# A scale vector loaded as rows, two small jobs moved to ScalarE, and other fill counts in an attention and MLP kernel

## The chip, the cores and the metric

The kernel runs on one core of a Trainium2 chip (trn2). The metric is the device time of one execution in microseconds (us), lower is better. Before the change it took 330.53 us (median of three runs, 330.24 to 331.06). A difference counts as faster or slower from 2% on, which is 6.6 us here.

## The reference

Nyström attention with 32 landmarks over (8 batches, 8 heads, 576 positions, 64), then one MLP block with a layer norm. The landmarks are means over 18 neighbours; the inverse of the 32x32 matrix comes from six iterations.

```python
A  = sm(q, k_lm);  Bm = sm(q_lm, k_lm);  C = sm(q_lm, k)     # sm: scaled softmax
Z  = Bm.T / (norm1(Bm) * norminf(Bm) + 1e-06)
for _ in range(6):
    Z = 2 * Z - Z @ Bm @ Z
x  = heads_side_by_side(A @ Z @ C @ v)                       # (8, 576, 512)
xn = (x - mean) / sqrt(var + 1e-06) * g_ln                   # g_ln: 512 numbers
return x + relu(xn @ w_ch1) @ w_ch2                          # 512 -> 2048 -> 512
```

## The kernel before

One program does both. TensorE (PE in the profile) has the most work. Attention runs in "sets" of batches; between two of its steps, `fill(n)` puts n pieces of the MLP's product stream into PE's order, so that PE has work while the other engines finish a step. At the very start there is no MLP work yet, and `warm(...)` issues products of zeros instead. The MLP works on groups of four blocks of 128 rows: `psh` is the first product of a block group, `pso` the second. `pscv` is C @ v, `psb` the scores of the landmarks, with which a set's iterations begin, and `psy` the last product of attention; `pszc` is the last product of the iterations, `zcbd` what VectorE makes of it as the input of `psy`; `st` and `ebd` are VectorE's tiles between the iterations' products, and `xblk` is a block of attention's result. `xn` is the normalised input, and `xnT` its turned copy, made by PE for the first groups and by a transposing DMA later.

The scale vector g is folded into W1. It is needed with one number for each partition, and it is loaded that way, as a 128x4 tile in pieces of 4 bytes, in the queue of SyncE (SP) behind the loads of q, k and v for the first batch:

```python
load_qk(0)
load_v(0)
g_sb = wpool.tile([P, KCH], FP32, name="g_sb")
keep(nc.sync.dma_start(out=g_sb[:], in_=moe_g_ln.rearrange("(c p) -> p c", p=P)))
...
def cast_v(b):                                   # GpSimd, both halves
    natv_of[b] = natv = natv_buf[b % NV]
    for u in range(U):
        pool.tensor_copy(out=natv[:, 2 * u:2 * u + 2, :, 0:D], in_=raw[b]["v", u][:])
...
def scale_w1(i, by=(0, 1, 2, 3)):                # W1 * g: a quarter on VectorE, the rest on GpSimd
    for c in by:
        o, i_ = w1_16[:, c, ts(i, W1N)], w1_stg[i, c // 2][:, ts(c % 2, W1N)]
        if c == 0:
            dve.tensor_scalar(out=o, in0=i_, scalar1=g_sb[:, c:c + 1], scalar2=None, op0=ALU.mult)
        else:
            pool.tensor_scalar(out=o, in0=i_, scalar1=g_sb[:, c:c + 1], scalar2=0.0,
                               op0=ALU.mult, op1=ALU.add)
```

The turned copies, the stores of the results and the later loads share one queue, SyncE's, which issues one after another:

```python
def center(j):                                   # GpSimd makes xn of block j, then it is turned
    ...
    pool.tensor_scalar(out=xn_of[j][:], in0=x_blk[j][:], scalar1=1.0, scalar2=negm, ...)
    turn_by_dma(j)

def turn_by_dma(j):
    ...
    keep(nc.sync.dma_start(out=xnTs[g][:, :, ts(u, P)], in_=xn_of.pop(j)[:], transpose=True))
    turned[g].append(j)

def store(j, ot, cols=ds(0, DM), queues=(nc.sync, nc.sync)):
    for i in range(2):
        ...                                      # two half-stores of block j
```

The first unit and the fill counts (cut):

```python
for it in range(6):                              # the six iterations of the first batch
    run(a0)                                      # one step of attention
    warm(1, 512)                                 # a product of zeros
    if it == 5:
        scale_w1(0, (0,))                        # VectorE scales the first part of W1
...
counts = [[8, 13, 9] + 6 * [7] + [5] + 3 * [6] + 2 * [9],                       # set 2
          [10, 10, 9, 9, 9, 9] + [9, 9, 8, 8, 8, 8] + [8] + [8, 8, 6, 5] + 6 * [9],   # set 3+4
          ...]
```

The softmax here doesn't subtract the row's maximum and nothing guards it: scores larger than these inputs give would overflow.

Of the kernel before, what the change touches and what calls it, by code (L numbers as in the profile page):

```python
# [10 lines left out]
FP32 = mybir.dt.float32  # L11
UINT32 = mybir.dt.uint32
AF = mybir.ActivationFunctionType
# [3 lines left out]
P = 128  # L17
# [3 lines left out]
def kernel(  # L21
# [10 lines left out]
    nc = tc.nc  # L32

    B, H, S, D = q.shape
    DM = H * D
# [5 lines left out]
    KCH = DM // P  # L41
# [10 lines left out]
        name=nc.get_next_instruction_name(), act_func_set_id=6, ins=[], outs=[]))  # L52

    const = ctx.enter_context(tc.tile_pool(name="const", bufs=1))
    wpool = ctx.enter_context(tc.tile_pool(name="wpool", bufs=1))
    stage = ctx.enter_context(tc.tile_pool(name="stage", bufs=6))
    nat = ctx.enter_context(tc.tile_pool(name="nat", bufs=8))


    keep = tc.keep_in_program_order  # L60
# [8 lines left out]
    dve, pool, scalar = Ordered(nc.vector), Ordered(nc.gpsimd), Ordered(nc.scalar)  # L69
    act = scalar.activation  # L70

    def MM(o, l, r, rb=0, cb=0, start=True, stop=True, skip=False):
        keep(nc.tensor.matmul(o, l, r, start=start, stop=stop, tile_position=(rb, cb),  # L73
                              skip_group_check=(skip or cb != 0)))

    def TR(o, i_, idn):
        keep(nc.tensor.matmul(o, i_, idn, is_transpose=True, tile_position=(0, 0)))
# [9 lines left out]
    raw = {0: {}, 1: {}}  # L87
# [26 lines left out]
    def cast_v(b):  # L114
# [4 lines that stand above are left out]
    nat_tiles, natv_of = {}, {}  # L119
# [1 line left out]
    load_qk(0)  # L121
    load_v(0)
    g_sb = wpool.tile([P, KCH], FP32, name="g_sb")
    keep(nc.sync.dma_start(out=g_sb[:], in_=moe_g_ln.rearrange("(c p) -> p c", p=P)))

    zeros = const.tile([P, 128], FP16, name="zeros")
    nc.vector.memset(zeros[:], 0.0)

    ident16 = const.tile([P, P], FP16, name="ident16")
    make_identity(nc, ident16)  # L130


    pm16 = const.tile([P, 64], FP16, name="pm16")
# [38 lines left out]
    natv_buf = []  # L172
# [7 lines left out]
        zcbd_buf.append(t)  # L180


    cast_v(0)
    bones = const.tile([P, 4, 32], FP16, name="bones")
    for u in range(U):
        for nm in ("q", "k"):
# [13 lines left out]
    w1_16 = wpool.tile([P, KCH, HID], FP16, name="w1_16")  # L200
    w2_16 = wpool.tile([P, MCH, DM], FP16, name="w2_16")
    w1_src = moe_w_ch1.rearrange("(c p) f -> p c f", p=P)
    xpool = ctx.enter_context(tc.tile_pool(name="xpool", bufs=16))

    W1N = 256
    w1_stg = {}
# [11 lines left out]
    def scale_w1(i, by=(0, 1, 2, 3)):  # L218
        for c in by:
            o, i_ = w1_16[:, c, ts(i, W1N)], w1_stg[i, c // 2][:, ts(c % 2, W1N)]  # L220
            if c == 0:
                dve.tensor_scalar(out=o, in0=i_, scalar1=g_sb[:, c:c + 1],
                                  scalar2=None, op0=ALU.mult)
            else:
                pool.tensor_scalar(out=o, in0=i_, scalar1=g_sb[:, c:c + 1],
                                   scalar2=0.0, op0=ALU.mult, op1=ALU.add)
# [37 lines left out]
    psM = ctx.enter_context(tc.tile_pool(name="psM", bufs=3, space=bass.MemoryType.PSUM))  # L264


    def warm(n, cols):
        idle = psM.tile([P, 512], FP32, name="idle", tag="pm")
        for _ in range(n):
            MM(idle[:, 0:cols], zeros[:], zeros[:, None, :].broadcast_to([P, cols // P, P]))  # L270
# [596 lines left out]
    def mlp():  # L867
        for g in range(NGRP):
            mlp_at[0] = g
            hT = mhT.tile([P, MCH, 512], FP16, name="hT", tag="hT")  # L870
            if g == 0:
                for u in (0, 2):
                    if u == 0:
                        for i in range(2):
                            transpose_block(0, i)
                            yield True
                    for m0 in range(0, MCH, 2):
                        if u == 0 and m0 in (6, 10):
                            transpose_block(0, 2 if m0 == 6 else 3)
                            yield True  # L880
                        if u == 0 and m0 < MCH - 6:
                            scale_w1(m0 // 2 + 3)
                        psh = psM.tile([P, 2, 256], FP32, name="psh", tag="pm")
                        for m in range(2):
                            for c in range(KCH):
                                MM(psh[:, m, :], w1_16[:, c, ts(m0 + m, P)],
                                   xnTs[0][:, c, ds(P * u, 256)],
                                   start=(c == 0), stop=(c == KCH - 1), skip=True)
                                if c == 1 or (c == 3 and m == 0):
                                    yield True  # L890
                        act(hT[:, m0:m0 + 2, ds(P * u, 256)], psh[:], AF.Relu)
                        yield True
# [52 lines left out]
    def run(*who):  # L945
        for a in who:
            next(a)
# [5 lines left out]
    run(a0)  # L953
    warm(1, 512)
    run(a0)
    warm(1, 512)
    run(a0)
    warm(2, 512)
    for it in range(6):
        run(a0)  # L960
        warm(1, 512)
        if it == 5:
            scale_w1(0, (0,))
    run(a0)
# [3 lines left out]
    run(a1)  # L968
    warm(1, 512)
    scale_w1(0, (1, 2, 3))  # L970
    fill(1)
    warm(2, 512)
# [57 lines left out]
    for _ in range(2):  # L1030
# [1 line left out]


    counts = [[8, 13, 9] + 6 * [7] + [5] + 3 * [6] + 2 * [9],
              [10, 10, 9, 9, 9, 9] + [9, 9, 8, 8, 8, 8] + [8] + [8, 8, 6, 5] + 6 * [9],
              [12, 12, 15, 15, 15, 13] + 6 * [11] + [10] + 10 * [8],
              [14, 21, 21] + 6 * [10] + [10] + 5 * [9]]
    for c, after, count in zip(sets, sets[1:] + [None], counts):
# [46 lines left out]
```

## Time and profile before

| | before |
|---|---|
| median, three runs | 330.53 us |
| profiled execution, span | 328.4 us |
| PE busy | 314.6 us of the span |
| first `psy` (first product with attention's result) | 22.10 us |
| GpSimd's last `xn` of group 3 ends | 137.03 us |
| its turned copy is issued / PE's `psh` of group 3 starts | 139.19 / 142.17 us |
| last VectorE step starts | 324.44 us |

In a timeline of SyncE's queue the columns are start, length of the issue, queue, line, operation, out<-in, how many.

```profile
136.57 1.21 SPq L861 DMA_TRANSPOSE xnT<-xn  x1
137.87 1.23 SPq L820 DMA_DIRECT2D out_dram<-ot  x2
139.19 1.26 SPq L861 DMA_TRANSPOSE xnT<-xn  x1
```

GpSimd had finished xn of block 15 at 137.03. The queue was issuing the copy of block 14 then, and after it two half-stores, and only at 139.19 the copy of block 15: 2.16 us after its input was ready.

### The profile page before, as it was taken

How to read it: one execution, taken by the hardware profiler on the slowest of the kernel's cores; microseconds unless marked ns; L12 is line 12 of the kernel's file. 1: busy time of each engine (PE TensorE's matmuls, PEld its weight loads, DVE VectorE, ACT ScalarE, POOL GpSimd, SP SyncE). 2: the span in 40 equal slices, each digit the busy share in tenths (PEclk: the TensorE clock that was granted, in tenths of full speed). 3: DMA queues.
4: the chain of work that ended last, by engine and by line, in shares of the span. 5: the costliest groups of instructions: out<-in, count | busy, mean ns of one | idle time of the engine just before them, and what ended most of it. 6: DMA issues, size and time to landing. Idle time of an engine off the chain costs nothing.

```text
span 328.4 us, 8241 instructions
## 1 busy us (share of the span) xinstructions
PE 314.6 (96%) x3408; PEld 163.0 (50%) x3408; DVE 176.7 (54%) x396; ACT 150.9 (46%) x304; POOL 154.6 (47%) x240
## 2 busy tenths in 40 slices
PE   8879899999999999989999999999999999999995
PEld 8537764454445544434545445454444444444443
DVE  2658869879966588864228568822557120010012
ACT  2426762739961561867304664364046107305600
POOL 3489889999999999989900025200014000000000
PEclk9999999999999999999999999999999999999999
DMA  7999999998598683698022203230242125032023
GB/s 276 350 361 360 383 401 291 317 359 250 212 209 226 186 225 109 163 278 128 4 66 59 43 16 80 66 66 2 64 103 27 32 64 98 0 72 60 0 49 79
DMA packets 36917, 50.34 MB, mean 153 GB/s; under 512 B 18320, under 2 KB 22672, under 8 KB 36880
## 3 DMA queue, kind: packets, MB, share of 16 engines
q1 hardware_dynamic: 36720, 49.69, 53.1%
q8 instruction: 26, 0.43, 0.6%
q10 hardware_dynamic: 160, 0.13, 0.2%
q14 instruction: 11, 0.09, 0.1%
HBM read 36.70 MB, written 9.44 MB: 141 GB/s over the span
## 4 chain that ended last, share of the span: by engine, by line
PE 58%; POOL 17%; DVE 6%; DMA 4%; issue 3%; ACT 2%; SPq 0%; POOLq 0%
PE psh L73 27%; PE pso L73 25%; POOL asum L67 9%; POOL nat L67 4%; POOL natv L67 2%; DMA out_dram<-ot 2%; POOL xn L67 2%; PE psy L73 1%; ACT xn L67 1%; DMA stg<-in_v_dram 1%; PE pscv L73 1%; DVE xT L67 1%; DVE ebd L67 1%; POOL s L67 1%; DMA xnT<-xn 1%
## 5 line engine op out<-in xcount | busy, mean ns | idle before, releaser
L73 PE MATMUL psh<-xnT,w 128*128 128x512 f16 (+1 forms) x640 | 134.2, 358 | 1.0 <-DMA xnT<-xn 1.0
L73 PE MATMUL pso<-w,hT 128*128 128x512 f16 (+1 forms) x592 | 133.0, 374 | 0.0
L67 ACT ACTIVATE hT<-psh 128x512 f16<-128x512 f32 x144 | 84.7, 597 | 94.8 <-PE psh L73 94.6
L73 PEld LDWEIGHTS <-w 128*128 128x128 f16 x640 | 59.4, 98 | 56.0 <-issue 3.0
L73 PEld LDWEIGHTS <-hT 128*128 128x128 f16 x592 | 56.0, 98 | 57.8 <-issue 0.9
L67 DVE SCALAR_TENSOR_TENSOR ot<-pso,rstd,xblk 128x512 f32<-128x512 f32 (+1 forms) x37 | 27.1, 732 | 79.0 <-PE pso L73 78.9
L67 POOL CAST nat<-stg 128x1152 f16<-128x1152 f32 x28 | 32.9, 1185 | 3.8 <-DMA stg<-in_k_dram 1.2
L67 POOL TENSOR_TENSOR asum<-asum 128x256 f32<-128x256 f32 (+2 forms) x54 | 28.3, 523 | 4.2
L67 DVE TENSOR_TENSOR xblk<-psy,rcpd 128x512 f32<-128x512 f32 (+1 forms) x40 | 27.6, 691 | 1.7
L67 POOL TENSOR_TENSOR asum<-nat 128x576 f32<-128x576 f16 x18 | 24.9, 1381 | 1.5
L67 DVE SCALAR_TENSOR_TENSOR st<-st,psn 128x192 f16<-128x192 f16 (+3 forms) x36 | 14.2, 395 | 19.1 <-PE psn L73 19.1
L67 POOL TENSOR_SCALAR xn<-xblk,mvg 128x512 f16<-128x512 f32 x14 | 9.6, 695 | 30.3 <-ACT junk L67 30.3
L67 POOL CAST natv<-stg 128x1152 f16<-128x1152 f32 x16 | 18.1, 1150 | 9.6 <-DMA stg<-in_v_dram 9.6
L67 POOL TENSOR_SCALAR negm<-mvg 128x1 f32<-128x1 f32 x14 | 2.7, 191 | 41.7 <-DVE mvg L67 40.2
L67 DVE TENSOR_TENSOR ebd<-st,mask 128x256 f16<-128x256 f16 (+1 forms) x30 | 21.4, 715 | 1.0
L67 DVE STREAM_TRANSPOSE xT<-nat 128x576 uint32<-128x576 uint32 x24 | 18.2, 760 | 0.8 <-POOL nat L67 0.8
L73 PE MATMUL psy<-zcbd,ea 128*128 128x260 f16 (+1 forms) x80 | 15.9, 276 | 1.3 <-DVE zcbd L67 1.1
L67 ACT ACTIVATE ea<-psea 128x576 f16<-128x576 f32 x12 | 7.2, 648 | 17.8 <-PE psea L73 17.8
L73 PE MATMUL idle<-zeros 128*128 128x128 f16 (+2 forms) x82 | 14.0, 325 | 1.1 <-DVE eps_ln L167 1.1
L73 PEld LDWEIGHTS <-ea 128*128 128x128 f16 (+1 forms) x80 | 7.3, 100 | 11.9 <-issue 4.2
L67 DVE RECIPROCAL rcpd<-psy 128x8 f32<-128x8 f32 (+1 forms) x40 | 7.8, 195 | 9.9 <-PE psy L73 9.6
L67 ACT ACTIVATE junk<-xblk 128x512 f16<-128x512 f32 x14 | 8.8, 625 | 9.3 <-DVE xblk L67 9.1
(109 smaller groups left out, 265.5 us busy)
## 6 DMA issues: line engine op xcount, KB each, us to landing
stg<-in_q_dram SPq DMA_DIRECT2D x16, 576.0 KB, 6.2
stg<-in_k_dram SPq DMA_DIRECT2D x16, 576.0 KB, 6.0
out_dram<-ot SPq DMA_DIRECT2D x70, 128.0 KB, 2.4
stg<-in_v_dram SPq DMA_DIRECT2D x10, 576.0 KB, 8.2
w1stg<-in_moe_w_ch_dram SPq DMA_DIRECT2D x16, 256.0 KB, 6.0
w2stg<-in_moe_w_ch_dram SPq DMA_DIRECT2D x16, 256.0 KB, 5.4
stg<-in_v_dram SPq DMA_DIRECT2D x12, 288.0 KB, 5.7
xnT<-xn SPq DMA_TRANSPOSE x28, 3.2
```

The lines of the kernel that those rows point to most:

```text
L67: return lambda *args, **kw: keep(getattr(self.engine, op)(*args, **kw))
L73: keep(nc.tensor.matmul(o, l, r, start=start, stop=stop, tile_position=(rb, cb), skip_group_check=(skip or cb != 0)))
```

## The change

The intent: free the DMA engines of a load in 512 small pieces, take two short jobs off GpSimd's and VectorE's order in the opening, and shift MLP products in the set of batches 3 and 4. The tile `g_rows` borrows a buffer of a pool that had to move to an earlier place for it.

```diff
-    keep(nc.sync.dma_start(out=g_sb[:], in_=moe_g_ln.rearrange("(c p) -> p c", p=P)))
+    g_rows = xpool.tile([P, DM], FP32, name="g_rows", tag="xblk")[0:KCH, 0:P]
+    keep(nc.sync.dma_start(out=g_rows, in_=moe_g_ln.rearrange("(c p) -> c p", p=P)))
...
+    ident4 = const.tile([KCH, KCH], FP32, name="ident4")
+    nc.gpsimd.tensor_copy(out=ident4[:], in_=ident16[0:KCH, 0:KCH])
...
-    cast_v(0)
+    natv_of[0] = natv_buf[0]
+    pool.tensor_copy(out=natv_buf[0][:, 0:2, :, 0:D], in_=raw[0]["v", 0][:])
+    pool.tensor_copy(out=natv_buf[0][:, 2, :, 0:D], in_=raw[0]["v", 1][:, 0])
...
-            if c == 0:
+            if c == 0 and i == 0:
+                act(o, i_, AF.Copy, scale=g_sb[:, c:c + 1])
+            elif c == 0:
...
     warm(1, 512)
     run(a0)
+    scalar.copy(natv_buf[0][:, 3, :, 0:D], raw[0]["v", 1][:, 1])
...
     for it in range(6):
         run(a0)
         warm(1, 512)
+        if it == 2:
+            psg = psM.tile([P, KCH], FP32, name="psg", tag="pm")
+            TR(psg[:], g_rows, ident4[:])
+            scalar.copy(g_sb[:], psg[:])
...
-              [10, 10, 9, 9, 9, 9] + [9, 9, 8, 8, 8, 8] + [8] + [8, 8, 6, 5] + 6 * [9],
+              [10, 9, 9, 9, 9, 8] + [8, 9, 9, 8, 8, 8] + [8] + [8, 7, 5, 4] + 6 * [9],
```

## The prediction

> **What bounds the kernel now.** I read the page first, then the busy time by stretch, the timeline of the first 30 us, and the chain of waits. The page says TensorE (PE) is the bound:
>
> ```profile
> span 328.4 us, 8241 instructions
> PE 314.6 (96%) x3408; PEld 163.0 (50%) x3408; DVE 176.7 (54%) x396; ACT 150.9 (46%) x304; POOL 154.6 (47%) x240
> ```
>
> PE is idle for 328.4 - 314.6 = 13.8 us. The stretches say where (columns: the stretch, its length, busy time of PE, PEld, DVE, ACT and POOL with instructions, clock, DMA share, GB/s):
>
> ```profile
> 10.00:11.00 1.00, 0.77 (x18) 0.63 (x17) 0.47 (x2) 0.71 (x1) 0.00 (x0) 1.00 1.03 408
> 11.00:12.00 1.00, 1.00 (x22) 0.62 (x21) 1.00 (x3) 0.00 (x0) 0.91 (x1) 1.00 0.58 151
> 12.00:13.00 1.00, 1.00 (x40) 0.68 (x37) 0.75 (x4) 0.76 (x2) 0.24 (x1) 1.00 0.64 197
> 13.00:14.00 1.00, 0.69 (x46) 0.58 (x46) 0.49 (x3) 0.64 (x2) 0.61 (x1) 1.00 1.02 394
> ...
> 140.00:150.00 10.00, 8.96 (x67) 3.86 (x72) 6.01 (x13) 6.66 (x16) 8.78 (x13) 1.00 1.15 238
> 150.00:170.00 20.00, 20.00 (x472) 10.05 (x457) 6.16 (x16) 7.38 (x14) 13.32 (x21) 1.00 0.25 58
> 170.00:200.00 30.00, 30.00 (x225) 14.54 (x223) 20.10 (x43) 15.70 (x31) 3.48 (x6) 1.00 0.23 49
> 200.00:250.00 50.00, 50.00 (x470) 23.93 (x468) 27.87 (x69) 20.07 (x41) 7.34 (x17) 1.00 0.32 62
> ```
>
> Two things to see. From 150 us PE has no gap until its last product, and a tail of about 4 us follows it (the last VectorE step starts at 324.44). So a saving counts only if it brings the PE work after 142 us forward. And the DMA engines, which run near 400 GB/s in the opening, drop to 151 and 197 GB/s between 11 and 13 us.
>
> The chain of waits (start, length, what) shows what holds PE at 142 us. GpSimd (POOL) is on it without a break from about 80 us, then a turned copy by DMA, then PE:
>
> ```profile
> 134.60 0.72 POOL natv L67
> ...
> 135.67 1.37 POOL xn L67 x2
> 137.03 2.16 POOL natv L67 x2
> 139.19 2.84 DMA xnT<-xn
> 142.04 0.14 issue
> 142.17 1.02 PE psh L73 x4
> ```
>
> PE waits 1.04 us there. GpSimd is busy almost without a wait from 51.8 us to then. Before 51.8 us it keeps pace with the loads, and those run back to back from 13 us on.
>
> **What the Trainium skill says.** "DMA: Bandwidth & Descriptors", section "Rules for kernel authors": a strided last dimension "Lowers to one descriptor per element"; its opening table puts the smallest line-rate transfer at 512 B. The old load of g is such a case, 128 partitions by 4 columns = 512 pieces of 4 B, only 2 KB in all; the rows are 4 pieces of 512 B. The trace agrees: it took 9.7 us to land, and the dip sits where the queue reaches it. "TensorE: Matmul & The Clock Gate", section "Part 4: PE-mode transpose", says that a transpose on PE is a product with an identity and ends in PSUM, so a copy must follow; in this trace one 128x128 f16 transpose shows 219 ns, and none in f32 is there. "ScalarE: Activation LUTs", section "Rules for kernel authors", gives VectorE the plain multiplications, as faster per element; here a scaling of 128x256 takes VectorE 0.56 us in the opening, so the move is not for speed of the operation but for VectorE's order.
>
> **The change, part by part.**
>
> Scale vector as rows. The dip is worth (408 - 151) + (408 - 197) = 468 KB, and 468 / 408 = 1.15 us. The next loads are in the same queue, so everything from the second v on should land up to 1.15 us sooner. GpSimd's casts and scalings to 51.8 us follow it; its dense stretch to 139 us follows them. Added: one small f32 transpose on PE and a copy on ScalarE, in the middle of the six iterations of the first unit. I estimate 0.1 to 0.2 us on the path, from the 219 ns above and a weight load of 98 ns, partly under the 0.43 us that PE's weight load waits there.
>
> First v. These lines of the timeline (start, length, engine, what) bear on this part and the next:
>
> ```profile
> 13.39 1.15 POOL L67 CAST natv<-stg 128x1152 f16<-128x1152 f32 x1 [1.16 <-DMA stg<-in_v_dram]
> ...
> 20.22 0.24 PE L73 MATMUL pszc<-st,bm 32*32 32x64 f16 x8
> ...
> 21.10 0.56 DVE L67 TENSOR_SCALAR w<-w1stg,g_sb 128x256 f16<-128x256 f32 x1 [0.93 <-DMA w1stg<-in_moe_w_ch_dram]
> ...
> 21.57 0.87 DVE L67 SCALAR_TENSOR_TENSOR zcbd<-pszc,cinv,mask 128x256 f16<-128x256 f32 x2
> 22.10 0.66 PE L73 MATMUL psy<-zcbd,ea 128*128 128x260 f16 x2 [1.11 <-DVE zcbd L67]
> ```
>
> PE's second half of pscv starts at 14.59, after the cast. Now GpSimd does half of that cast, 0.6 us, and ScalarE the other, but only after its two exponentials, which end at 13.64; at 648 ns for 128x576 it ends near 14.3. PE gains 0.25 us. ScalarE sets this time: with v landing 1.15 us sooner GpSimd alone would end at about 12.3 + 1.15 = 13.5. This part may therefore be worth nothing or slightly less than nothing once the load is mended.
>
> Scaling of W1 on ScalarE. VectorE, in order, waits at 20.17 for W1 to land, scales, and only then makes zcbd, whose input is ready at 20.46. That is 21.57 - 20.5 = 1.07 us of PE time lost. ScalarE is idle then (its next work came 5.97 us later), and its 128x64 takes 212 ns and 128x512 597 ns, so 128x256 is estimated at 0.38 us: beside other work. PE's first real products thus come 1.07 + 0.25 - 0.15 = about 1.2 us sooner.
>
> Fill counts. The last hunk is called fewer zero products, but the program has the same zero products before and after. What it lowers is the number of MLP products placed between attention steps of batches 3 and 4, by 5 in sum (6 fewer, 1 more). A 128x512 product costs 0.216 us (64 in 13.81), so those steps come up to 1.08 us earlier against the MLP and the five products run later. No PE time is saved. The order of engines shows GpSimd's and the DMA queue's order around 142 us unchanged, so the turned copy stays bound by GpSimd.
>
> **Sum.** PE front 1.2 us sooner, GpSimd 1.15 us sooner. At 142 us PE would arrive about 1.2 us earlier, less 0.2 us for one more pair of psy products placed ahead of it, and the turned copy about 1.15 us earlier: the wait stays near 1 us and the smaller shift, 1.15 us, goes through to the end. Around 122 to 125 us PE also waits 0.25 + 0.67 us for VectorE's ebd; the new counts put one more product behind the third iteration, worth perhaps 0.2 us. 330.53 - 1.15 - 0.2 = 329.2 us.
>
> **The rivals.** (a) GpSimd does not pass its 1.15 us on: its dense stretch has about 80 us of work whose lengths vary (the same sum takes 1.27 to 1.7 us), and the loads could wait for freed buffers instead. For it: GpSimd is 9.2 to 9.7 of 10 busy. Then PE waits about 2 us at 142 instead of 1, and the time stays at 330.3 to 330.5. Against it: the opening loads are back to back and their buffers are freed by the same engines, also sooner. (b) The counts do more than I give them: attention results sooner, both waits gone: another 0.9 + 1.0 us, 327.4 us. Against it: the scalings xn before the wait follow GpSimd's casts, not PE. (c) A new wait on the path, from the f32 transpose or ScalarE's late cast: up to 0.5 us of the front, 329.7 us. (d) VectorE's order with fewer products between makes PE wait where it had none at 95 to 118 us: at most some 0.2 us at each of two steps.
>
> **Range and chances.** Most weight is on 1.15 to 1.4 us; (a), (c) and (d) pull up to 330.2, (b) down to 328.2. All of it is under 0.8%, far inside 2%, which is 6.6 us.
>
> **What would show it.** Right: no dip in GB/s between 11 and 13 us; the second natv cast and the later casts about 1.1 us earlier; zcbd straight after pszc, psy at about 20.9; the psh after the turned copy near 141.0 with about 1 us of wait; PE without gaps after 150. Wrong: the dip stays with 4 pieces, so it was not g's; or GpSimd's last casts still end near 139; or the wait at 142 is gone. If the front moves by over 1 us and the end by under 0.5, the step from front to end is false.

## The result, and the profile after

The changed kernel took 329.42 us (median of six runs, 328.48 to 329.57) against 330.30 us for the kernel before in the same six rounds (329.90 to 331.06). The ratio is 0.9967, with a 95% interval of 0.9951 to 0.9983: a real gain of about a third of a per cent, "same" by the 2% rule. A ratio here is the mean time of one kernel's fast runs over that of the other's fast runs of the same rounds, so it is not quite the ratio of the medians quoted beside it.

The two profiled executions took 330.07 and 329.57 us, only 0.50 us apart; the traces account for that much and no more. The page after:

```profile
span 327.9 us, 8249 instructions
PE 314.7 (96%) x3409; PEld 162.3 (50%) x3409; DVE 175.7 (54%) x395; ACT 152.7 (47%) x307; POOL 153.3 (47%) x241
```

PE is busy for 314.7 us, against 314.6 before, with one product more, the small transpose. So the work is the same, and what changed is waiting. The stretches, with the columns as in the prediction:

```profile
10.00:11.00 1.00, 0.78 (x19) 0.78 (x19) 0.47 (x3) 0.54 (x1) 0.07 (x1) 1.00 1.09 411
11.00:12.00 1.00, 1.00 (x28) 0.63 (x26) 0.98 (x2) 0.08 (x1) 1.00 (x1) 1.00 1.01 379
12.00:13.00 1.00, 0.87 (x37) 0.53 (x29) 0.74 (x4) 0.82 (x3) 0.08 (x1) 1.00 1.04 392
...
150.00:170.00 20.00, 20.00 (x428) 9.94 (x426) 7.24 (x19) 7.19 (x14) 12.06 (x18) 1.00 0.19 48
```

The dip is gone: 379 and 392 GB/s where there were 151 and 197. From 150 us on PE still has no gap. Now the timeline of the opening (start, length, engine, line, what, and in brackets the idle time before it with what ended it):

```profile
13.49 0.68 ACT L68 CAST natv<-stg 128x576 f16<-128x576 f32 x1
13.52 0.67 POOL L68 CAST natv<-stg 128x576 f16<-128x576 f32 x1 [1.44 <-DMA stg<-in_v_dram]
...
15.03 1.15 POOL L68 CAST nat<-stg 128x1152 f16<-128x1152 f32 x1 [0.84 <-DMA stg<-in_q_dram]
...
20.16 0.88 DVE L68 SCALAR_TENSOR_TENSOR zcbd<-pszc,cinv,mask 128x256 f16<-128x256 f32 x2 [0.34 <-PE pszc L74]
...
20.40 0.51 ACT L68 ACTIVATE w<-w1stg,g_sb 128x256 f16<-128x256 f32 x1 [2.40 <-DMA w1stg<-in_moe_w_ch_dram]
20.70 0.89 PE L74 MATMUL psy<-zcbd,ea 128*128 128x260 f16 x4
```

Three things are to be seen. VectorE's zcbd follows pszc without W1's scaling before it, and `psy` starts at 20.70 instead of 22.10. ScalarE does the scaling meanwhile. But the second half of v landed no earlier: its cast starts at 13.52, against 13.39 before, although the DMA engines were at full rate. Its load is issued ahead of g's in both kernels (at 3.50 and 4.01 us in the kernel before), so g's pieces never stood in front of it. And the first cast that follows, that of q for the next batch, starts at 15.03 instead of 15.35: only 0.32 us sooner, and half of that is a difference between the two executions that is there earlier (the first cast of v starts at 10.93 instead of 11.09).

The chain of waits that ended last, at 142 us, and SyncE's queue there:

```profile
134.86 1.36 POOL xn L68 x2
136.22 2.16 POOL natv L68 x2
138.38 3.20 DMA xnT<-xn
...
141.71 1.89 PE psh L74 x8
```

```profile
135.75 1.20 SPq L870 DMA_TRANSPOSE xnT<-xn  x1
137.04 1.24 SPq L829 DMA_DIRECT2D out_dram<-ot  x2
138.38 1.25 SPq L870 DMA_TRANSPOSE xnT<-xn  x1
```

GpSimd finishes at 136.22 instead of 137.03, and the copy is issued at 138.38 instead of 139.19: both 0.81 us sooner. The `psh` that needs the copy starts at 141.71 instead of 142.17, only 0.46 us sooner, after a wait of PE that grew from 1.04 to 1.42 us. The last VectorE step starts at 323.96 instead of 324.44, 0.48 us sooner. In both traces the chain puts the 2.16 us between the end of xn and the issue down to GpSimd's next casts (natv). The queue's timeline contradicts it: GpSimd is done, and the issue waits for its turn behind the copy of block 14 and two half-stores.

I call the start of this `psh` the gate. In all eleven timed kernels and repeats, and in the two kernels of the comparison, the start of the last VectorE step less the start of this `psh` lies between 182.1 and 182.4 us. So what a kernel saves in its profiled execution is what it saves at the gate.

### The profile page after: what moved, and what is told of

It reads as the page before. It is cut to its first block, busy times and chain, and to the rows that moved or that the text cites. A ratio compares the mean times of both kernels' runs of the same rounds, so it can differ in the third digit from the quotient of the medians.

```text
span 327.9 us, 8249 instructions
## 1 busy us (share of the span) xinstructions
PE 314.7 (96%) x3409; PEld 162.3 (50%) x3409; DVE 175.7 (54%) x395; ACT 152.7 (47%) x307; POOL 153.3 (47%) x241
## 4 chain that ended last, share of the span: by engine, by line
PE 56%; POOL 22%; DMA 7%; issue 2%; ACT 2%; DVE 1%; SPq 0%; POOLq 0%
PE psh L74 26%; PE pso L74 25%; POOL asum L68 11%; POOL nat L68 6%; POOL natv L68 3%; DMA stg<-in_q_dram 3%; POOL xn L68 2%; DMA w2stg<-in_moe_w_ch_dram 2%; POOL s L68 1%; PE psy L74 1%; PE pscv L74 1%; DMA stg<-in_v_dram 1%; DMA stg<-in_k_dram 1%; DMA xnT<-xn 1%; ACT xn L68 1%
## 5 line engine op out<-in xcount | busy, mean ns | idle before, releaser
L68 POOL TENSOR_TENSOR asum<-nat 128x576 f32<-128x576 f16 x18 | 23.4, 1299 | 1.5
L68 POOL CAST natv<-stg 128x1152 f16<-128x1152 f32 (+1 forms) x16 | 17.6, 1119 | 9.6 <-DMA stg<-in_v_dram 9.6
L68 DVE TENSOR_TENSOR ebd<-st,mask 128x256 f16<-128x256 f16 (+1 forms) x30 | 20.7, 690 | 1.0
L68 DVE BATCH_NORM_STATS2 st<-xblk 128x6 f32<-128x512 f32 x18 | 12.4, 688 | 0.5
```

The source lines that it names most:

```text
L68: return lambda *args, **kw: keep(getattr(self.engine, op)(*args, **kw))
```

## The experiments

There were three sets that were timed in rounds. All outputs are right. Each set had its own runs of the kernel before on the same chip (medians of eleven runs: 330.68, 330.35 and 330.69 us). In some of the expectations the time at which the disturbance of the first loads was expected, 12.3 us, is counted from another zero than the traces'; read it as 10 to 12 us of the profile.

### Which part of the change does it

**Rows only**: the kernel before with g as rows, the turn on PE and its copy, nothing else.

```diff
 before.py
-    keep(nc.sync.dma_start(out=g_sb[:], in_=...rearrange("(c p) -> p c", p=P)))
+    keep(nc.sync.dma_start(out=g_rows, in_=...rearrange("(c p) -> c p", p=P)))
+    ident4 = ...
+        if it == 2: TR(psg[:], g_rows, ident4[:]); scalar.copy(g_sb[:], psg[:])
```

> Only the rows of g with the turn on PE; casts, scaling and fill counts as before. Theory A (the end follows GpSimd's chain through the wait at 142 us): the dip in GB/s at 11 to 13 us is gone, GpSimd's scalings of W1 start 0.5 to 0.8 us earlier, and the time falls by 0.4 to 0.9 us against before. Rival B (the end follows PE's front): the front moves by about 0.4 us because VectorE still scales before zcbd, and the time falls by 0.3 us or less.

**Columns kept**: the changed kernel with the old load of g (no turn, no `ident4`).

```diff
 after.py
-    keep(nc.sync.dma_start(out=g_rows, in_=...rearrange("(c p) -> c p", p=P)))
+    keep(nc.sync.dma_start(out=g_sb[:], in_=...rearrange("(c p) -> p c", p=P)))
-        if it == 2: TR(...); scalar.copy(...)
```

> The whole change except the rows: g is loaded as 512 pieces as before. Theory A: PE's first psy comes about 1.3 us earlier, GpSimd's W1 scalings do not move, PE waits over 1.5 us at the turned copy near 142, and the time falls by 0.3 us or less. Rival B: the time falls by 0.8 us or more.

**Front only**: the changed kernel with the old counts. **Counts only**: the kernel before with the new counts.

```diff
 after.py (front only); counts only is the same line the other way round, in before.py
-              [10, 9, 9, 9, 9, 8] + [8, 9, 9, 8, 8, 8] + [8] + [8, 7, 5, 4] + 6 * [9],
+              [10, 10, 9, 9, 9, 9] + [9, 9, 8, 8, 8, 8] + [8] + [8, 8, 6, 5] + 6 * [9],
```

> The changed kernel with the old fill counts. Theory A: the counts save no PE time and the turned copy is bound by GpSimd, so the time is that of the changed kernel, 0.8 to 1.3 us under before. Rival C (the counts carry the gain): 0.5 us or less under before.

> The kernel before with the new fill counts alone. Theory A: within 0.3 us of before, the wait at 142 us still 1.0 to 1.4 us. Rival C: 0.5 us or more under before.

| run | median us | ratio to before, 95% | last xn ends | copy issued | gate |
|---|---|---|---|---|---|
| before (profile) | 330.30 | 1 | 137.03 | 139.19 | 142.17 |
| after (profile) | 329.42 | 0.9967 (0.9951 to 0.9983) | 136.22 | 138.38 | 141.71 |
| rows only | 330.59 | 1.0010 (0.998 to 1.004) | 136.38 | 138.53 | 142.61 |
| columns kept | 330.54 | 0.9999 (0.9976 to 1.0023) | 137.10 | 139.26 | 142.87 |
| front only | 329.96 | 0.9985 (0.996 to 1.001) | 136.21 | 138.36 | 141.74 |
| counts only | 331.04 | 1.0003 (0.9987 to 1.0019) | 137.43 | 139.59 | 143.28 |

The load of g sorts these kernels as far as the copy's issue, though narrowly, and their gates overlap. The five kernels with rows and without a changed queue order (after, rows only, front only, and two of the next section) put the end of the last xn at 136.4 on average and the gate at 142.00; the three with columns (before, columns kept, counts only) at 137.2 and 142.77. Over all thirteen traces, those with a changed queue order included, the last xn ends at 136.29 on average with rows and at 137.09 with columns; single kernels overlap (136.93 with rows, 136.68 with columns). So on average GpSimd does carry the earlier loads through its whole dense stretch, and the averages at the gate differ by 0.78 us.

Columns kept has a front nearly as early as the changed kernel's (first `psy` at 20.88) and yet no gain in time. Its trace does not show where an early front ends, though: PE was done with the work ahead of the gate at 141.17, against 141.13 before, so the lead was lost on the way. Front only shows it: there PE was done at 139.19, 1.94 us sooner than before, then waited 2.55 us for the copy, and the gate came only 0.43 us sooner. Front only's 0.72 us in the medians lies between its two expectations, and its interval includes no gain.

Rows only is the miss. Its xn and its copy come nearly as early as in the changed kernel, and PE's front is no later than before (first `psy` at 21.40), so the gate should have been earlier than before too. It came at 142.61. In this execution the turned copy was the reason: from its issue to the `psh` it took 4.08 us.

```profile
138.53 1.24 SPq L866 DMA_TRANSPOSE xnT<-xn  x1
...
142.61 1.02 PE L74 MATMUL psh<-xnT,w 128*128 128x512 f16 x4 [2.12 <-DMA xnT<-xn]
```

The same distance was 2.98 us before, 3.33 after, 3.61 and 3.38 in columns kept and front only and 3.69 in counts only. What makes it vary by 1.1 us was not found. The six timed runs of rows only show no gain either, and only one of them has a trace. So that rows alone bring nothing is what the timed runs say; whether a slow copy explains all of them is not shown.

### The changed kernel again, and the queue at the gate

If the queue's order holds the last copy for 2.16 us, then issuing the copies of blocks 14 and 15 ahead of the stores and the next load of q should move the gate. A store or a load that comes up between the copies of blocks 13 and 15 is held, and put out after the copy of 15:

```diff
 after.py
+    held = [None]
+    def release():
+        jobs, held[0] = held[0], None
+        for f in jobs:
+            f()
     def store(j, ot, cols=ds(0, DM), queues=(nc.sync, nc.sync)):
+        if held[0] is not None:
+            held[0].append(lambda: store(j, ot, cols, queues))
+            return
 ...                                             # turn_by_dma
         turned[g].append(j)
+        if j == 13:
+            held[0] = []
+        if j == 15:
+            release()
 ...                                             # next_load
-        if to_load:
+        if held[0] is not None:
+            held[0].append(next_load)
+        elif to_load:
```

> The changed kernel again, as the yardstick for the runs of this call: 0.8 to 1.3 us under before; v of the second half lands near 13.5 us again if the 16 KB instruction fetch at 12.3 us is what holds it, near 12.5 us if that was a chance of one run; wait at the turned copy near 142 us 1.0 to 1.5 us.

> The changed kernel, but the DMA queue issues the turned copies of blocks 14 and 15 straight after that of block 13; the q load and the two stores that stood between are issued after them. Theory A (PE has over 1 us in hand, the turned copy of block 15 holds it, and it is held by the queue's order): the last turned copy is issued 1.2 to 1.8 us earlier, the wait of 1.4 us at 142 us falls under 0.4 us, and the time falls by 0.9 to 1.5 us against the changed kernel. Rival: the copies take as much longer as they start sooner, or the wait comes back later: less than 0.4 us.

The third of this set takes the split cast of v back: GpSimd casts all of it.

```diff
 after.py
-    pool.tensor_copy(out=natv_buf[0][:, 2, :, 0:D], in_=raw[0]["v", 1][:, 0])
+    cast_v(0)                                   # GpSimd, both halves
-    scalar.copy(natv_buf[0][:, 3, :, 0:D], raw[0]["v", 1][:, 1])
```

> The changed kernel with GpSimd casting all of the first v again. If the second half of v lands near 13.5 us, its cast ends at 14.65 instead of 14.2 and PE's second half of pscv starts 0.4 us later. Theory A: GpSimd is paced by loads after it, so the time is within 0.3 us of the changed kernel. Rival B (PE's front sets the end): 0.4 us slower than the changed kernel.

| run | median us | ratio to before, 95% | first psy | last xn ends | copy issued | gate |
|---|---|---|---|---|---|---|
| after again | 329.20 | 0.9961 (0.9936 to 0.9986) | 20.86 | 136.99 | 139.14 | 142.51 |
| turned first | 328.76 | 0.9947 (0.9922 to 0.9973) | 21.13 | 136.01 | 137.32 | 140.61 |
| no cast on ScalarE | 329.26 | 0.9968 (0.994 to 0.9995) | 21.04 | 136.13 | 138.28 | 141.41 |

The repeat confirms the gain of the change. (Its profiled run was the slowest of its six, 330.23 us, and its gate is late accordingly; one execution of a kernel differs from another by about as much as the changes compared here, which is why times from rounds decide and not one trace.) With the turned copies first, the copy goes out 1.31 us after its input instead of about 2.16, PE does not wait for it at all, and the gate is at 140.61. One half-store still stood between the two copies. The time was expected to fall by 0.9 to 1.5 us against the changed kernel; the medians differ by 0.44 us and the intervals overlap, so this is a miss. The edit also takes the load of q and a half-store away from in front of the copy. Where the traces show the landing, the copy landed 2.84 to 3.56 us after its issue in three kernels without the edit and 2.46 to 3.10 us in the four of the next section that have it; no run separates this from the order of the issues.

Without ScalarE's cast the first `psy` is 0.34 us later than in the changed kernel (0.18 us later than in its repeat, and earlier than in turned first), and neither the gate nor the time shows a loss: PE arrives at the gate too early in both.

### With the queue mended: which part counts then

Four kernels: the order of the queue alone on the kernel before; on columns kept; on front only (rows, ScalarE's jobs, old counts); and turned first once more. Each edit is the one shown above.

> The kernel before with nothing changed but the queue's order: the turned copies of blocks 14 and 15 straight after that of block 13. Theory A (one wait for the turned copy of block 15 sets the end): the wait of 1.04 us at 142 us is gone, PE starts that psh at 141.1, and the time falls by 0.7 to 1.1 us against before, as much as the whole change under study gave. Rival B: the front of PE sets the end and this gives 0.3 us or less.

> The change without the rows of g, which alone gave nothing against before (ratio 0.9999), and with the turned copies first. Theory A: its earlier front of PE was hidden by the wait of 1.70 us at 142 us; with the copy about 1.7 us sooner that wait falls under 0.4 us and the time falls by 1.2 to 1.8 us against before. If the front had been lost elsewhere: 0.8 us or less.

> The changed kernel with the turned copies first and the old fill counts. Theory A: the counts save no PE time once the wait is gone, so within 0.4 us of the changed kernel with the turned copies first. Rival C: the counts still matter, 0.5 us or more slower than that.

> The changed kernel with the turned copies first again, as the yardstick of this call: 1.5 to 2.2 us under before, no wait over 0.3 us for a turned copy near 141 us.

| run | median us | ratio to before, 95% | psb of set 3+4 | copy issued | gate | from psb to gate |
|---|---|---|---|---|---|---|
| before + order | 329.14 | 0.9946 (0.9911 to 0.998) | 95.29 | 138.54 | 141.18 | 45.89 |
| columns kept + order | 329.25 | 0.9956 (0.9921 to 0.9991) | 94.84 | 137.99 | 141.28 | 46.44 |
| front only + order | 328.18 | 0.9917 (0.988 to 0.9953) | 93.50 | 136.76 | 139.39 | 45.89 |
| turned first again | 328.71 | 0.9931 (0.9893 to 0.9968) | 93.73 | 138.25 | 141.31 | 47.25 (47.58 less its wait of 0.33 for the copy) |

The order of the queue alone, on the kernel before, is worth as much as the whole change: 0.9946 against 0.9967 and 0.9961. The changed opening with the mended queue and the old counts has the lowest median, 328.18 us, and the lowest ratio, 0.9917. Against turned first again it is 0.53 us faster in the medians, where the expectation had the two within 0.4 us or the other way round; the intervals of all four overlap, so the lead over the other three is not clear. Its profiled run (327.33 us) was the fastest of its six. In its trace the queue and PE look like this at the gate:

```profile
133.04 2.95 SPq L880 DMA_TRANSPOSE xnT<-xn  x2
136.08 0.59 SPq L839 DMA_DIRECT2D out_dram<-ot  x1
136.76 1.24 SPq L880 DMA_TRANSPOSE xnT<-xn  x1
```

```profile
138.31 1.24 PE L74 MATMUL pso<-w,hT 128*128 128x512 f16 x5
...
139.39 1.03 PE L74 MATMUL psh<-xnT,w 128*128 128x512 f16 x4
```

PE goes from `pso` to `psh` without a bracket of idle time: the gate is gone, and PE's own earlier opening shows at 139.39 against 141.18 in the kernel before with the same order. The pair that should show the front alone, columns kept against before, does not: in that execution the front's lead of 1.64 us at the first `psy` (20.70 against 22.34) had shrunk to 0.45 us at the psb of set 3+4 (94.84 against 95.29). With the same code up to there, columns kept without the order had 93.89, so this is spread between executions, and whether the front alone counts with columns is left open.

The last column tells what the counts cost (`psb` of set 3+4 is the mark at about 95 us at which that set's counts begin to matter). Taken in the same way for all thirteen traces, less the wait at the gate, PE needs 45.89 to 46.20 us from the psb of set 3+4 to the gate in the five kernels with the old counts. With the new ones it needs 46.33 to 46.44 us in three (counts only, turned first, columns kept + order) and 47.25 to 47.31 us in five (columns kept, the changed kernel and its repeat, no cast on ScalarE, turned first again). One more pair of `psy` products before the gate accounts for 0.22 us of that. The five also have waits of PE, about 0.4 us for VectorE's xblk and 0.2 to 0.3 us for its st, that no kernel with the old counts shows; the rest was not traced. While PE has to wait at the gate anyway, this cost is free.

### Why the second half of v did not land sooner

In the changed kernel the two halves of v land 2.59 us apart, whereas the neighbouring loads of the same size land about 1.5 us apart. The DMA view of the stretch from 10 to 11 us (queue, kind: packets, MB, share of 16 engines) has a packet of another queue, one of the fetches of instructions:

```profile
q8 instruction: 1, 0.02, 6.7%
```

6.7% of sixteen engines for 1 us is one engine for 1.07 us. A load waits for its slowest engine, so it lands about that much later. In the kernel before the fetch lies between 11 and 12 us, inside the dip of g. In all thirteen traces with this warm-up a fetch of 1.03 to 1.13 us starts between 10.6 and 11.4 us, and the cast of the second half of v starts between 13.39 and 13.85. If this is right, moving the fetch must move the late landing. Fewer products of zeros in the warm-up, each larger, shift when it is made:

```diff
 after.py
-    warm(50, 128)
+    warm(10, 128)
+    warm(10, 512)
```

> The changed kernel with 20 warm-up products ahead of the first tile in place of 50 (10 of 128 and 10 of 512 columns, about the same time), which takes 60 instructions out ahead of the opening. If the 16 KB instruction fetch at about 12.3 us, which keeps one DMA engine for 1.07 us, is what made the second half of v land 0.5 to 1.1 us late, the fetch comes about 1 us later, that half of v lands 1.5 to 1.6 us after the first half (it was 2.3 to 2.6), and one of the next two loads shows a gap of 2.0 to 2.6 us in its place. If the delay is the loads' own, the gap of 2.3 to 2.6 us stays at the second half of v. No difference in time is expected that one look can show.

```profile
12.84 0.67 POOL L68 CAST natv<-stg 128x576 f16<-128x576 f32 x1 [0.37 <-DMA stg<-in_v_dram]
14.37 1.15 POOL L68 CAST nat<-stg 128x1152 f16<-128x1152 f32 x1 [0.86 <-DMA stg<-in_q_dram]
16.61 1.14 POOL L68 CAST nat<-stg 128x1152 f16<-128x1152 f32 x1 [1.10 <-DMA stg<-in_k_dram]
16.87 0.24 PE L74 MATMUL pscv<-natv,ect 64*32 64x65 f16 x8 [1.98 <-issue]
```

The fetch is now between 14 and 15 us (again one packet, 7.0% of that stretch). The halves of v start their casts 1.52 us apart (11.32 and 12.84), q follows after 1.53, and the late one is the load of k, 2.24 us after q. The late landing went along with the fetch, in this one execution.

As a kernel this run is worse: 338.46 us against 330.38 on the same chip, in one look, so its state is unknown. PE waited 1.98 us at pscv for something that the profile names only "issue", and its clock, the third figure from the end of the next line, was at half from 18 to 26 us:

```profile
18.00:20.00 2.00, 2.00 (x29) 0.50 (x25) 0.71 (x2) 0.65 (x1) 1.62 (x2) 0.50 1.10 350
```

PE had been busy for 0.73 and 1.13 us in the two stretches of 2 us before. The Trainium skill, "TensorE: Matmul & The Clock Gate", section "What's actually happening", has the clock fall to half after an idle window of about 3.4 us. The trace agrees only in part: the fall follows 4 us of which PE worked 1.9, but no single wait was longer than 1.98 us. What PE waited for, perhaps the very instructions that were fetched late, isn't shown.

## Why the prediction was right

The time was right, and in the main so was the mechanism, two chains that meet at one gate. Two terms of the sum, the load's and the counts', were too large, and the queue that ended the second chain was missed.

- **"The wait stays near 1 us and the smaller shift goes through to the end."** Right in outcome, and partly by luck. The wait at 142 us stayed (1.42 us), and the end moved with the gate to 0.02 us (0.48 and 0.46). PE was done with the work ahead of the gate 0.84 us sooner (140.29 against 141.13), and the copy was issued 0.81 us sooner. But PE's lead had been 2.06 us at the psb of set 3+4, and the new counts and waits took 1.22 us of it on the way, which the prediction did not have. By the prediction's own sign ("if the front moves by over 1 us and the end by under 0.5, the step from front to end is false") that step failed in the profiled pair, 1.40 and 0.48 us; in the timed medians the end moved by 0.9 us or more. The rival that GpSimd loses its gain on the way is refuted by its last xn, which comes 0.81 us sooner, and 0.80 us sooner on average over the thirteen traces.
- **"468 / 408 = 1.15 us."** The term was too large. The dip went, but GpSimd's first scaling of W1 starts 0.75 us sooner on average (20.78 in eight runs with rows, 21.53 in five with columns), and the gate moves by 0.78. That "everything from the second v on" should come sooner was a misreading: v's load stands ahead of g's in the queue, and its second half landed no sooner. Nor were the 9.7 us that g took to land a sign of its pieces, as the load of q issued after it took 9.9 us; the dip was. The cast of q behind it starts 0.47 us sooner on average. In both kernels a fetch of instructions delays loads at the same place. The last experiment shows that by moving it; that the dip had partly hidden this delay is inferred. The Trainium skill, "DMA: Bandwidth & Descriptors", section "Why a DMA increments its semaphore by 16 and not by 1", says that up to 16 engines finish a DMA independently and that only the full count means the data has landed. The trace agrees: one engine kept busy for 1.07 us made the load land about 1.1 us late. Bytes lost are not landing time lost.
- **"Worth perhaps 0.2 us"** for the counts. Not shown. Alone they give 1.0003; with them and without them the changed kernel has the same gate (141.71 and 141.74). The medians of the two (329.2 to 329.4 with, 329.96 without) come from different sets and their intervals overlap. The wait of 0.25 us for ebd that they were to cover did vanish in the changed kernel, but from the psb to the gate PE needed 47.27 us in the changed kernel and 46.20 in front only, and the wait at the gate hid that. The rival of new waits of PE between 95 and 118 us was thus partly right: one of 0.27 us came at 110 us, and two of about 0.2 us at 130 to 132 us.
- **"PE front 1.2 us sooner."** It was 1.40 us at the first `psy`, of which about 0.15 us lay between the two executions already at 11 us, and 2.06 us at the psb of set 3+4, as waits between 28 and 50 us shrank too. Of that, 1.22 us was lost before the gate and 0.38 us at it. What the split cast of v gave is not settled: without it `psy` came 0.34 us later than in the changed kernel, but turned first, with it, came later still, as ScalarE's half ended only at 14.64 us there. In that execution ScalarE did set the time, as the prediction feared. No time shows a difference.
- **"The turned copy stays bound by GpSimd."** Only half true, and the step I would now read differently. The copy waited 2.16 us in the queue behind other issues, more than the whole predicted gain of 1.35 us, plainly in the timeline of SyncE's queue of the kernel before. The chain labelled it with GpSimd's name and I took the label.
- **The small costs.** ScalarE's scaling of W1 took 0.51 us, not 0.38, beside other work. The f32 transpose cost a weight load of 0.13, a product of 0.22 and a copy of 0.16 us; no delay of the iterations beside it was seen.
- **The sum, 1.35 us.** The medians and ratios of the changed kernel and its repeat show 0.9 to 1.3 us, the gates 0.78 on average, and the profiled pair 0.48: the sum was on the high side, within the range. In that pair the turned copy took 3.33 us from issue to use instead of 2.98, which took back 0.35 of GpSimd's 0.81 us; why that time varies stays open. The timed runs alone do not show which part carries the gain: rows alone, the change without the rows, and the counts alone gave nothing clear. That the earlier load, together with the opening, carries it rests on the traces.

## What to carry to other kernels

Where two chains meet at one wait, a saving in either is worth only what the later one allows, so look first at what happens in the last microseconds before the meeting: here the order of a few issues in one DMA queue was worth as much as a reworked opening. When a chain says that an engine holds a transfer, check the queue's own timeline for what it was issuing in that time. And take a gap in DMA throughput as no more than an upper estimate of what closing it brings: here a gap of 1.15 us was worth about 0.75, and another disturbance, the fetch, lay under it.

## What the Trainium skill lacked or had wrong

- "Runtime: NRT & Kernel Launch", section "Instruction fetch mechanics", says that instructions are fetched in blocks of 16 KiB through a DMA queue of the sequencer's own, and calls the cost mostly hidden. The traces agree on the block (one packet of 0.02 MB); the page lacks that a fetch takes one DMA engine for about 1.1 us (1.07 in the changed kernel) and that a load of another queue lands about that much later (2.59 us after the load before it instead of about 1.5).
- "DMA: Bandwidth & Descriptors" has no figure for what a load in 4-byte pieces costs the loads behind it. Here 512 such pieces cost an estimated 1.15 us of the engines' throughput (from the dip in GB/s), and on average GpSimd's work on the loads behind it came 0.75 us later for it.
- The same page has no time measured on trn2 for the issue of a transposing DMA from SBUF of this size (its cycle counts for such issues stand in the part on trn3), and none for its way to the consumer. Here a 128x512 f16 copy at the gate took 1.24 to 1.27 us of the issuing queue, against about 0.6 us for a load of q or a half-store, and 2.98 to 4.08 us from issue to the product that waited for it.
- No page has the point that a chain of waits can put a queue's own issue time down to the compute engine that works meanwhile: 2.16 us in both kernels here. This is a point on reading the profile, not on the chip.
